# The first expert's token list in token order, two of its row tiles gathered before the last dense store, its first four slices split 256+128

## The chip, the cores and the metric

One core of a Trainium2 chip. The metric is the device time of one execution in microseconds (us). It has five engines with queues of their own, each worked off in order: PE (TensorE, matmuls), DVE (VectorE), ACT (ScalarE), POOL (GpSimd) and SP (SyncE, which here only issues transfers).

## The reference, cut to what matters

Three stages follow one another on 3072 tokens of 512 numbers:

```python
x = attention(q, k, v, mem_k, mem_v)         # windows of 32 queries, 8 heads of 64
h = x @ w_in; g = np.maximum(0.01 * h, h)    # dense: 512 -> 2048 -> 512
x = g @ w_out
logits = x @ w_gate                          # 8 experts, cap = 3072 // 8 = 384 tokens each
# (token, expert) pairs from the highest logit down: a token goes to the first expert
# of its pairs that is not full yet, until every token has one
for e in range(8):
    out[mask[e]] = np.maximum(x[mask[e]] @ w1[e], 0.0) @ w2[e]     # 512 -> 1024 -> 512
```

Every expert ends with exactly 384 tokens. Which expert fills first, and with which tokens, depends on the logits of all tokens.

## The kernel before, in words

**Order.** Nothing is written in its final order by hand. `Plan` holds every instruction (or small group) as an operation with an engine, a planned duration, a key (lower goes first) and what it depends on. A list scheduler goes through them with these durations and so sets the order of each engine's queue; the hardware then runs the queues with semaphores. A planned duration that is off costs nothing by itself, it only changes orders.

**Dense stage.** Tokens go in 8 blocks of 384 (`TB`), that is 3 row tiles of 128 (`TT`), 24 row tiles in all. The hidden 2048 are 16 slices of 128. A slice is `gemm1` (12 matmuls of 384 columns: each operand is a high and a low part, three products of four depth pieces) and `gemm2` (9 matmuls of 512 columns, three for each row tile). The plan numbers slices s = 16 * block + slice, and `gemm2` of slice s comes two slices behind `gemm1`. Attention units of 96 queries run between the slices of the block before; for the last block they are spread by `EARLY`.

**Towards the routing.** The routing needs all logits, and these can be had without the last `gemm2`s: from slice S6 = 7*16 - ND on, `gate` multiplies the hidden slice with the folded matrix w_out @ w_gate (two matmuls of 384 columns a slice, L994; the last three slices by 8-column matmuls, L1004), and what was summed up to then gives its part by dot products on DVE (`x2_part`, `x2_gate`, L1069). So the `gemm2`s from S6 on are put off (hidden slices kept in `gd`, in `spare` and in parts of `win`): those of the last ND slices of block 6, and all 16 of block 7, row tile by row tile (21, 22, 23). PE has them to do while the search runs.

**Search.** `search(p)` finds the expert that fills p-th and its tokens. It is a chain of small DVE steps and small PE steps (`count` L315, `base` L337, `sums`, `before_it`): each step waits for the one before. `fill` marks the tokens, `ranks`, `slots`, `places`, `parts`, `tokens`, `indices` turn them into a list of 384 token numbers (`tail(p)`). The slot of a token in the list is the number of list tokens in lower partitions plus those in earlier row tiles of its own partition.

**Experts.** `gather` fetches the list's rows from `x2d` (dense results in DRAM, stored by `x2_out` L1053, L1054) with three indirect transfers of 128 rows from POOL (L478), one for each row tile of the list. `transpose` (L483, 4 matmuls a row tile), `xhi` (ACT, L486) and `xlo` (DVE, L490) make the operand. An expert has 8 slices of `gemm1` (L614) and `gemm2` (L637), the same shapes as the dense ones. Its weights are loaded by SP (L587) and split in high and low by ACT (L595) and DVE (L597); those of the first expert go through the `x` buffers and into `win` (`room`), piece f once the dense slices that lie there are used up (`roomy`).

In the first expert every gather waits for every dense store (`xready`) and for `open_experts`, and every first matmul of `gemm1` waits for all three row tiles (`XT[p]`). What follows the last dense matmul is filled on PE by up to 40 matmuls of the identity (L667).

Of the kernel before, what the change touches and what calls it, by code (L numbers as in the profile page):

```python
# [67 lines left out]
class Plan:  # L68
# [37 lines left out]
    def dma(self, us, fn, deps=(), use=(), after=(), key=None, queue=0.45):  # L106
        q = self.op({"Q": queue}, fn, deps, use, after, key)
        d = self.op({"D": us}, None, (), use, (), key)
        self.dep(d, [q], lat=1.1)
        return d  # L110

    def run(self):
# [13 lines left out]
        while todo:  # L126
# [29 lines left out]
            todo -= 1  # L156
            if o.fn:
# [55 lines left out]
def phase2(tc, P, C, ident, L, x2d, we, out, ps_h, ps_o, ps_y, pools, lready, xready, open_pools, open_experts, room, roomy, before):  # L213
# [17 lines left out]
    SW = 0.12  # L231
# [171 lines left out]
    def fill(p):  # L403
# [4 lines left out]
        fx = r["fx"] = rt([128, NTILE + 1], BF, "fx", 2)  # L408
# [16 lines left out]
    def ranks(p):  # L425
        r = R[p]
        r["ps"] = pools["ps_t"].tile([128, 1], FT, name="pt")
        nc.tensor.matmul(r["ps"], C[0]["tri"], r["fx"][:, NTILE:], start=True, stop=True)

    def slots(p):  # L430

        r = R[p]
        b = rt([128, NTILE], FT, "sb")
        a = rt([128, NTILE], I16, "sl")
        V.tensor_scalar(b, r["fx"][:, :NTILE], r["ps"], 32.0, op0=OP.add, op1=OP.add)
# [45 lines left out]
    def transpose(b, x):  # L481
        for d in range(KD):
            nc.tensor.transpose(b.t[:, d * 128:(d + 1) * 128], x.t[:, d * 128:(d + 1) * 128], ident)  # L483
# [17 lines left out]
    r_xt = [ring(2, [128, KD, TB], FR, f"xt{n}") for n in "hl"]  # L501
    r_g = [ring(3, [128, TB], FR, f"eg{n}") for n in "hl"]
# [10 lines left out]
    def search(p):  # L513
# [6 lines left out]
        for n in range(NL):  # L520
# [3 lines left out]
            o = small((0.047 if n < UPPER else 0.06) * W, lambda n=n: count(p, n), [o], late=late)  # L524
# [5 lines left out]
        o = small(0.17, lambda: sums(p), [o], late=late)  # L530
        o = P.op(("V", 1.9), lambda: which(p), [o])
        t = small(0.04, lambda: before_it(p), [o], late=late)
        o = P.op(("V", 0.8), lambda: above(p), [o])
        chain[:] = [P.op(("V", 0.72), lambda: full(p), [o, t])]
        filled[p] = P.op(("V", 0.5), lambda: fill(p), chain, key=-1000 + 10 * p + (1 if p else -1))
# [3 lines left out]
    def tail(p):  # L539
        P.key = -1000 + 10 * p + (1 if p else -1)  # L540
        late = SLACK if p else 0.0
        o = small(0.04, lambda: ranks(p), [filled[p], tchain], late=late)
        o = P.op(("V", 0.67), lambda: slots(p), [o])
        ts = [P.op(("V", 0.47), lambda: places(p), [o]), P.op(("V", 0.6), lambda: parts(p), [o])]
        o = small(0.53, lambda: tokens(p), ts, late=late)
# [3 lines left out]
        for i in range(TT):  # L549
            x = r_xg[i].take()  # L550
# [724 lines left out]
```

## Time and profile before

| | |
|---|---|
| median of 3 runs | 993.36 us (993.26 to 994.73) |
| the profiled execution | 995.56 us |
| its span on the core | 993.8 us |
| PE busy | 971.8 us (98%) |
| DVE busy | 768.8 us (77%) |
| ACT busy | 444.9 us (45%) |
| POOL busy | 130.7 us (13%) |
| mean granted PE clock | 0.997 |

The profile comes from one execution, 995.56 us long, of which 993.8 us are the span from its first to its last instruction. Times of rows are us from the span's start. Matmuls overlap: a 512-column matmul is listed with 0.39 us, and the next one begins 0.23 us later, so the pace is read from starts, not from durations, and a busy PE can still run filler.

### The profile page before, as it was taken

The numbers are of one execution on the slowest core, as the hardware profiler recorded it, in microseconds if no ns is written. First come the engines' busy times: TensorE is split into PE (matmuls) and PEld (weight loads), VectorE is DVE, ScalarE is ACT, GpSimd is POOL, SyncE is SP. The second block draws the span as 40 slices with busy tenths as digits, with TensorE's granted clock in tenths as the row PEclk, the third lists the DMA queues.
The fourth block names the chain that finished last, engine by engine and source line by source line (L and its number), as shares of the span: only waits on it lengthen the run. The fifth ranks groups of instructions, "written<-read, shape, count | busy, mean of one in ns | idle before, by whom it ended". The sixth has DMA issues, their size and how long they took to land.

```text
span 993.8 us, 17323 instructions
## 1 busy us (share of the span) xinstructions
PE 971.8 (98%) x6068; PEld 844.4 (85%) x6068; DVE 768.8 (77%) x2573; ACT 444.9 (45%) x1187; POOL 130.7 (13%) x145
## 2 busy tenths in 40 slices
PE   8899999999999999999999999998999999999997
PEld 7778888888888888888888889877888888888996
DVE  7899798698698689689778685579988989885710
ACT  7777634444444544444544433214425334334521
POOL 0577521000000000000000000001121112112211
PEclk9999999999999999999999999999999999999999
DMA  8567521111011111110120000024633625526600
GB/s 262 197 213 239 191 65 30 30 62 60 30 62 39 50 63 30 56 65 31 48 72 12 1 1 1 37 75 155 201 127 129 204 94 169 172 74 209 226 32 32
DMA packets 36327, 95.50 MB, mean 96 GB/s; under 512 B 4368, under 2 KB 8464, under 8 KB 36112
## 3 DMA queue, kind: packets, MB, share of 16 engines
q1 hardware_dynamic: 32256, 81.54, 24.6%
q0 software_dynamic: 3840, 12.59, 3.8%
q8 instruction: 48, 0.79, 0.3%
q14 instruction: 39, 0.32, 0.1%
q10 hardware_dynamic: 144, 0.26, 0.1%
HBM read 81.79 MB, written 12.58 MB: 95 GB/s over the span
## 4 chain that ended last, share of the span: by engine, by line
PE 83%; DVE 8%; issue 4%; ACT 1%; DMA 1%; POOL 1%; POOLq 0%; DVEq 0%; ACTq 0%; SPq 0%
PE po L1039 24%; PE ph L946 24%; PE ph L614 13%; PE po L637 11%; PE pa L828 3%; PE pa L898 2%; PE pa L871 2%; PE po L1094 2%; DVE junk L1069 2%; DVE wp L923 1%; DVE wa L925 1%; DMA wst<-in_w_dram 1%; PE pt L483 1%; DVE wp L922 1%; PE pc L315 1%
## 5 line engine op out<-in xcount | busy, mean ns | idle before, releaser
L1069 DVE CUSTOM_DVE_ANT_0 junk<-x,wgb 128x512 bf16<-128x512 f32 x296 | 207.5, 701 | 5.6 <-ACT x L1053 0.8
L954 ACT ACTIVATE gs<-ph 128x384 f32<-128x384 f32 x128 | 62.6, 489 | 196.9 <-PE ph L946 189.9
L1039 PE MATMUL po<-wouth,gh 128*128 128x512 f32 x336 | 136.4, 406 | 0.0
L955 DVE TENSOR_TENSOR gs<-ph,gs 128x384 f32<-128x384 f32 x128 | 71.1, 555 | 84.1 <-ACT gs L954 83.8
L1039 PE MATMUL po<-woutl,gh 128*128 128x512 f32 x336 | 133.7, 398 | 1.3 <-POOL woutl L930 1.3
L1039 PE MATMUL po<-wouth,gl 128*128 128x512 f32 x336 | 132.0, 395 | 0.6 <-POOL gl L957 0.6
L837 ACT ACTIVATE X<-X,st 96x128 f32<-96x128 f32 x248 | 96.8, 391 | 47.7 <-DVE st L832 47.4
L946 PE MATMUL ph<-x1h,winh 128*128 128x384 f32 x512 | 111.5, 339 | 0.0
L946 PE MATMUL ph<-x1h,winl 128*128 128x384 f32 x512 | 110.9, 337 | 0.1
L946 PE MATMUL ph<-x1l,winh 128*128 128x384 f32 x512 | 110.3, 336 | 0.0
L946 PEld LDWEIGHTS ph<-x1h,winh 128*128 128x128 f32 x512 | 91.7, 188 | 9.5
L620 ACT ACTIVATE egh<-ph 128x384 fp32r<-128x384 f32 x64 | 31.4, 491 | 150.5 <-PE ph L614 142.2
L946 PEld LDWEIGHTS ph<-x1h,winl 128*128 128x128 f32 x512 | 92.3, 188 | 1.4 <-POOL winl L930 0.4
L946 PEld LDWEIGHTS ph<-x1l,winh 128*128 128x128 f32 x512 | 91.2, 189 | 0.2
L1039 PEld LDWEIGHTS po<-wouth,gl 128*128 128x128 f32 x336 | 63.0, 188 | 15.4 <-POOL gl L957 1.7
L1039 PEld LDWEIGHTS po<-wouth,gh 128*128 128x128 f32 x336 | 63.1, 188 | 13.7
L1039 PEld LDWEIGHTS po<-woutl,gh 128*128 128x128 f32 x336 | 63.2, 188 | 12.9 <-POOL woutl L930 2.7
L956 ACT ACTIVATE gh<-gs 128x384 fp32r<-128x384 f32 x112 | 58.7, 524 | 34.1 <-DVE gs L955 33.9
L621 DVE SCALAR_TENSOR_TENSOR egl<-ph,egh 128x384 fp32r<-128x384 f32 x64 | 35.3, 551 | 44.0 <-ACT egh L620 43.7
L832 DVE CUSTOM_DVE_ANT_0 X<-pa,masks 96x128 f32<-96x128 f32 x232 | 56.3, 281 | 4.7 <-PE pa L828 4.7
L957 DVE TENSOR_TENSOR gl<-gs,gh 128x384 fp32r<-128x384 f32 x88 | 48.5, 551 | 10.7 <-ACT gh L956 10.6
L1154 POOL IOTA ij<- 128x128 int32 x1 | 0.2, 235 | 425.7 <-DVE L L1069 425.7
(245 smaller groups left out, 1911.5 us busy)
## 6 DMA issues: line engine op xcount, KB each, us to landing
west<-in_we_dram SPq DMA_DIRECT2D x56, 512.0 KB, 4.5
wst<-in_w_dram SPq DMA_DIRECT2D x32, 512.0 KB, 4.2
vt<-in_v_dram SPq DMA_DIRECT2D x30, 256.0 KB, 2.6
kt<-in_k_dram SPq DMA_DIRECT2D x30, 256.0 KB, 3.4
qt<-in_q_dram SPq DMA_DIRECT2D x31, 192.0 KB, 3.0
x2d<-x SPq DMA_DIRECT2D x21, 256.0 KB, 2.2
x<-in_we_dram SPq DMA_DIRECT2D x16, 256.0 KB, 2.7
wgb<-in_w_gate_t_dram SPq DMA_DIRECT2D x1, 2048.0 KB
```

The costliest lines, as they stand in the source:

```text
L614: nc.tensor.matmul(ph.t[:, :TB], w[a].t[:, k * 128:(k + 1) * 128], xs[x].t[:, k, :], start=(n == 0), stop=(n == 3 * KD - 1))
L621: b = P.op(("V", 0.47), lambda: V.scalar_tensor_tensor(gl.t, ph.t[:, :TB], 0.0, gh.t.bitcast(FT), op0=OP.max, op1=OP.subtract), [a], [ph, ...
L637: nc.tensor.matmul(ACC[p][i].t, l.t[:, 128 * i:128 * i + 128], w[a].t[:, 512:1024], start=(f == 0 and n == 0), stop=(f == NF - 1 and n == 2))
L832: V.tensor_tensor_reduce(out=X.t[:, h, :], in0=ps[h % 2].t[:QB, h // 2 * 128:h // 2 * 128 + 128], in1=masks[:, var, :], scale=-scale, scal ...
L837: S.activation(X.t[:, h, :], X.t[:, h, :], AF.Exp, bias=st.t[:, 0, h:h + 1], scale=-1.0, accum_out=st.t[:, 2, h:h + 1])
L946: nc.tensor.matmul(ph.t[:, :TB], win[wt][:, f, kk * 128:(kk + 1) * 128], xt.t[:, kk, :], start=(n == 0 and kk == 0), stop=(n == 2 and kk = ...
L954: o = P.op(("S", 0.37), lambda: S.activation(t.t, ph.t[:, :TB], AF.Copy, scale=0.01), [o], [ph, t], key=k)
L955: o = P.op(("V", 0.47), lambda: V.tensor_tensor(t.t, ph.t[:, :TB], t.t, op=OP.max), [o], [ph, t], key=k)
L956: x = P.op(("S", 0.42), lambda: S.activation(gh(), t.t, AF.Copy), [o, gd], [t, *gb], key=k)
L957: y = P.op({"V": 0.47} if j > 1 else {"V": 0.47, "G": 0.96} if j else {"G": 0.96}, lambda e=V if j > 1 else G: e.tensor_tensor(gl(), t.t, ...
L1039: nc.tensor.matmul(acc.t, lt()[:, sl], wout[wt][:, f, :], start=(f == 0 and n == 0), stop=(n == 2 and (f == NF - 1 or s == S6 - 1)), skip_ ...
L1069: V.tensor_tensor_reduce(out=pools["wgb"].tile([128, DM], BF, name="junk"), in0=x, in1=WGB[0][:, e, :], scale=1.0, scalar=0.0, op0=OP.mult ...
```

## The change

1. `ranks` and `slots` number the list by token: a matmul with ones gives the count of each row tile, a scan over the row tiles and a subtraction the tokens in earlier tiles, the matmul with the triangle the rank inside the tile. This holds for all eight lists. Slot s then has a token of at most 3071 - (383 - s), so the first 128 rows of a list lie in row tiles 0 to 21 and the next 128 in 0 to 22.
2. For the first expert, gathers 0 and 1 read only `x2d` up to row tiles 21 and 22, go to a free part of the `gd` buffers (`rows`) and wait neither for later stores nor for `open_experts`. Gather 2 is as before. `open_experts` waits for the two early transposes.
3. For the first expert, slices 0 to 3 run first for the columns of row tiles 0 and 1 (256), `gemm1` and `gemm2`, then for row tile 2 (128); slices 4 to 7 follow whole. Its operands and hidden slices use the dense buffers (`mlp` stays open).
4. The identity matmuls at L667 are gone. Those of the start (`warm`) take a bank of PSUM whose users have ended in the plan, or are left out.
5. ND goes from 3 to 8 (S6 from 109 to 104): five more slices of block 6 are put off and gated, and the last block's attention units lie 2.2 instead of 3.8 slices apart. The dot products of block 6 get a later key.
6. Weight loads of the first expert no longer wait for `roomy`; the splits do, pieces 0 to 2 only for the last `gemm1`, the others for the last dense matmul as well. Some planned durations of small PE steps are lower.

```diff
 def ranks(p):
-        r["ps"] = pools["ps_t"].tile([128, 1], FT, name="pt")
-        nc.tensor.matmul(r["ps"], C[0]["tri"], r["fx"][:, NTILE:], start=True, stop=True)
+        r["ps"] = pools["ps_t"].tile([128, 2, NTILE], FT, name="pt")
+        for n, x in enumerate(("ones", "tri")):
+            nc.tensor.matmul(r["ps"][:, n], C[0][x], r["F"], start=True, stop=True)
 def slots(p):
-        V.tensor_scalar(b, r["fx"][:, :NTILE], r["ps"], 32.0, op0=OP.add, op1=OP.add)
+        V.tensor_tensor_scan(fx, r["ps"][:, 0], c["zero"], 0.0, op0=OP.add, op1=OP.add)
+        V.tensor_tensor(fx, fx, r["ps"][:, 0], op=OP.subtract)
+        V.scalar_tensor_tensor(b, r["ps"][:, 1], 32.0, fx, op0=OP.add, op1=OP.add)
 def fill(p):
-        V.memset(fx[:, 0:1], 0.0)
-        V.tensor_tensor_scan(fx[:, 1:], r["F"], c["zero"], 0.0, op0=OP.add, op1=OP.add)
 def gather(p, i, x):
-        G.indirect_dma_start(out=x.t, out_offset=None, in_=x2d,
+        G.indirect_dma_start(out=x.t if p or i == TT - 1 else x.t[:, i * DM:(i + 1) * DM], out_offset=None, in_=x2d if p else x2d[:(NTILE - TT + 1 + i) * 128],
 def tail(p):
-            g = P.op(("G", 1.25), lambda i=i, x=x: gather(p, i, x), [o, xready, open_experts], [x])
+            early = p == 0 and i < TT - 1
+            g = P.op(("G", 1.25), lambda i=i, x=x: gather(p, i, x),
+                     [o, [d for t, d in xready if p or t < NTILE - TT + 1 + i], [] if early else open_experts], [x])
...
+            if early:
+                P.dep(open_experts, [o])
 def gemm1(p, f, lo=0, hi=TB):
-            t = [P.op(("T", 0.175), lambda n=n: mm(n), [o[0], XT[p], t], [ph, *w, *xs])]
+            t = [P.op(("T", {128: 0.112, 256: 0.122, TB: 0.178}[k]), lambda n=n: mm(n),
+                      [o[0], XT[p][lo // 128:hi // 128], t], [ph, *w, *xs])]
...
-    b, o = ps_o[0].take(), before
-    for n in range(40):
-        prev, o = o, P.op(("T", 0.22), lambda: None if b.gone else nc.tensor.matmul(
-            b.t[:, :128], ident, ident, start=True, stop=True), (), [b] if n == 0 else (), key=1e6)
-        P.dep(o, [prev], lat=0.15)
...
+        if p == 0:
+            for lo, hi in ((0, TB - 128), (TB - 128, TB)):
+                tiles = range(lo // 128, hi // 128)
+                for f in range(FA + 2):
+                    if f < FA:
+                        if lo == 0:
+                            load(p, f)
+                        gemm1(p, f, lo, hi)
+                    if f >= 2:
+                        gemm2(p, f - 2, tiles)
...
-    ND = 3
+    ND = 8
...
     def warm():
-        b = next((b for b in spots[::-1] if (b.tile or b is spots[0]) and not b.gone), None)
-        if b:
-            nc.tensor.matmul(b.t[:, 384:], ident, ident, start=True, stop=True)
+        for b in spots:
+            if (b.tile or b is spots[0]) and not b.gone and all(u.end and u.end < P.now - 0.05 for u in b.users):
+                nc.tensor.matmul(b.t[:, 384:], ident, ident, start=True, stop=True)
+                break
```

## Rows read from the trace of the kernel before

**Rows 1.** The page: PE's busy time, and the chain that ended last by engine.

```profile
PE 971.8 (98%) x6068; PEld 844.4 (85%) x6068; DVE 768.8 (77%) x2573; ACT 444.9 (45%) x1187; POOL 130.7 (13%) x145
...
PE 83%; DVE 8%; issue 4%; ACT 1%; DMA 1%; POOL 1%; POOLq 0%; DVEq 0%; ACTq 0%; SPq 0%
```

**Rows 2.** Timeline of PE, 669 to 684: start, us, instruction.

```profile
669.40 0.39 PE L1039 MATMUL po<-wouth,gl 128*128 128x512 f32 x1
...
678.17 0.60 PE L483 MATMUL pt<-ident,xg 128*128 128x128 f32 x4
...
683.05 0.96 PE L614 MATMUL ph<-xth,winh 128*128 128x384 f32 x4
```

**Rows 3.** Timeline of DVE, ACT, SP and POOL, 633 to 684.

```profile
633.14 0.18 DVE L1022 TENSOR_SCALAR L<-pl 128x24 f32<-128x24 f32 x1 [0.39 <-PE pl L1004]
...
657.82 0.60 ACT L1053 ACTIVATE x1h<-po 128x512 f32<-128x512 f32 x1 [12.99 <-PE po L1039]
...
664.74 0.70 DVE L475 TENSOR_TENSOR idx<-pt,ix 32x3 int32<-32x3 f32 x4
...
669.83 0.60 ACT L1053 ACTIVATE x1h<-po 128x512 f32<-128x512 f32 x1 [3.39 <-PE po L1039]
...
670.45 0.33 SPq L1054 DMA_DIRECT2D x2d<-x1h  x1
...
673.64 1.17 POOL L478 DMA_INDIRECT xg<-x2d,idx  x1 [73.55 <-DVE d L281]
...
682.42 0.58 ACT L486 ACTIVATE xth<-ph 128x512 fp32r<-128x512 f32 x1
...
683.17 0.68 DVE L490 TENSOR_TENSOR xtl<-ph,xth 128x512 fp32r<-128x512 f32 x1
```

**Rows 4.** Groups of PE instructions by line and shape, 669.63 to 683.05: busy us, mean ns.

```profile
L483 PE MATMUL ph<-ident,xg 128*128 128x128 f32 x8 | 1.3, 280 | 0.3 <-DMA xg<-x2d,idx 0.3
L315 PE MATMUL pc<-oh,cm 128*128 128x32 bf16 x18 | 0.9, 178 | 1.4 <-DVE cm L298 0.8 <-issue 0.6
L483 PE MATMUL pt<-ident,xg 128*128 128x128 f32 x4 | 0.6, 272 | 0.0
L337 PE MATMUL pb<-fl,ones 32*128 32x1 bf16 x3 | 0.5, 158 | 1.1 <-DVE fl L333 0.7 <-issue 0.3
L315 PE MATMUL pc<-oh,cm 128*128 128x16 bf16 x12 | 0.5, 170 | 0.0
```

**Rows 5.** Timeline of PE in the first expert: the pace of 384 and 512 columns.

```profile
698.38 0.85 PE L614 MATMUL ph<-xth,winl 128*128 128x384 f32 x4
699.08 0.85 PE L614 MATMUL ph<-xtl,winh 128*128 128x384 f32 x4
699.77 0.39 PE L637 MATMUL po<-winh,egh 128*128 128x512 f32 x1
700.00 0.40 PE L637 MATMUL po<-winl,egh 128*128 128x512 f32 x1
```

**Rows 6.** Groups of PE, 575 to 635: the put-off products of block 6.

```profile
L1039 PE MATMUL po<-wouth,gd 128*128 128x512 f32 x18 | 6.1, 395 | 0.0
```

**Rows 7.** Busy time by stretch: PE, PEld, DVE, ACT, POOL, then granted clock, DMA.

```profile
520.00:540.00 20.00, 20.00 (x129) 17.87 (x128) 18.85 (x63) 8.29 (x25) 0.00 (x0) 1.00 0.05 14
540.00:560.00 20.00, 20.00 (x129) 17.86 (x128) 16.95 (x59) 8.91 (x31) 0.00 (x0) 1.00 0.00 1
...
600.00:633.00 33.00, 33.00 (x187) 30.37 (x185) 14.46 (x45) 13.73 (x28) 0.10 (x1) 0.95 0.07 24
...
721.30:918.00 196.70, 194.97 (x1189) 163.94 (x1185) 162.99 (x587) 78.40 (x150) 34.94 (x47) 1.00 0.44 148
```

**Rows 8.** The same view over single microseconds: the granted clock.

```profile
628.00:629.00 1.00, 1.00 (x6) 1.00 (x6) 0.00 (x0) 0.00 (x0) 0.00 (x0) 0.73 0.21 78
...
631.00:632.00 1.00, 1.00 (x4) 0.75 (x3) 0.56 (x1) 0.38 (x2) 0.00 (x0) 0.56 0.00 0
```

**Rows 9.** Timeline of PE: the one wait of a later expert's start.

```profile
918.14 0.97 PE L614 MATMUL ph<-xth,winh 128*128 128x384 f32 x4 [1.15 <-ACT xth L486]
```

More of the change, by code (lines that the diff above doesn't have):

```diff
@@ L109, in dma @@
         self.dep(d, [q], lat=1.1)
+        d.queue = q
         return d
@@ L156, in run @@
             todo -= 1
+            self.now = t
             if o.fn:
@@ L523, in search @@
             o = P.op(("V", 0.08 + K * T * W / 1920), lambda n=n: compare(p, n), [o])
-            o = small((0.047 if n < UPPER else 0.06) * W, lambda n=n: count(p, n), [o], late=late)
+            o = small(0.026 * W, lambda n=n: count(p, n), [o], late=late)
             for m in range(K - 1):
@@ L607, in gemm1 @@
         xs = X[p]
+        c, k = slice(lo, hi), hi - lo
         ph = ps_h.take()
-        gh, gl = (r.take() for r in r_g)
+        gh, gl = (r.take() for r in (r_gb if lo else r_g))
         def mm(n):
             a, x = ((0, 0), (1, 0), (0, 1))[n // KD]
-            k = n % KD
-            nc.tensor.matmul(ph.t[:, :TB], w[a].t[:, k * 128:(k + 1) * 128], xs[x].t[:, k, :],
+            d = n % KD
+            nc.tensor.matmul(ph.t[:, :k], w[a].t[:, d * 128:(d + 1) * 128], xs[x].t[:, d, c],
                              start=(n == 0), stop=(n == 3 * KD - 1))
@@ L630, in gemm2, with mm @@
         w, o = W[p, f]
-        gh, gl, done = GL.pop(s)
-        if f == 0:
+        if f == 0 and p not in ACC:
             ACC[p] = [r.take() for r in ps_o]
-        def mm(i, n):
+        def mm(i, n, gh, gl, at):
             l, a = ((gh, 0), (gh, 1), (gl, 0))[n]
-            nc.tensor.matmul(ACC[p][i].t, l.t[:, 128 * i:128 * i + 128], w[a].t[:, 512:1024],
+            nc.tensor.matmul(ACC[p][i].t, l.t[:, at:at + 128], w[a].t[:, 512:1024],
                              start=(f == 0 and n == 0), stop=(f == NF - 1 and n == 2))
-        for i in range(TT):
+        for i in tiles:
+            gh, gl, at, done = GL.pop((s, i))
             if p == E - 1 and f >= NF - 2:
@@ L678, in phase2 @@
         tail(p)
-        for f in range(NF + 2):
-            if f < NF:
+        first = []
+        if p == 0:
[8 more added lines that the diff above has]
+                        gemm2(p, f - 2, tiles)
+            first = range(FA)
+        for f in range(NF):
+            if f not in first:
                 load(p, f)
@@ L683, in phase2 @@
             s = NF * p + f - 2
-            if f >= 2 or p > 0:
-                if f < NF:
-                    gemm2(*divmod(s, NF))
+            if s >= 0 and s not in first:
+                gemm2(*divmod(s, NF))
         if p == E - 1:
@@ L969, in gstore @@
         if n < 0:
-            b = [r_gd.take() for _ in range(2)]
-            return (lambda: b[0].t), (lambda: b[1].t), b, [ev["gd"]]
+            if n == -ND:
+                early.extend(r.take() for r in r_gd)
+            return (lambda: early[0].t[:, n + ND, :]), (lambda: early[1].t[:, n + ND, :]), early, [ev["gd"]]
         if n < KD:
```

94 lines of the change are left out of this document (50 added, 44 removed).

## The prediction

> **What bounds the kernel now.** I read the page first: PE is busy in nearly the whole span, and the chain that ended last runs through PE for 83% of it [rows 1]. So time is won where PE waits or does filler, and lost wherever PE gets more work. A busy share doesn't show filler, so next I followed the timeline of PE through the passage from the dense stage to the experts. The last dense matmul starts at 669.40; at the pace of 0.23 us for 512 columns [rows 5] the next could start at 669.63. The first matmul of an expert starts at 683.05 [rows 2]. These 13.4 us hold no dense and no expert product.
>
> The timelines of the other engines say why [rows 3]. The search of the first expert begins when the logits are complete, at 633.14, and its list is ready after the four steps at 664.74, so at 665.4: before the dense stage ends. What ends last is the store. ACT copies the last row tile at 669.83, SP issues its store at 670.45, the first gather starts at 673.64, its rows are turned by PE at 678.17 [rows 2], and the other two row tiles follow; ACT's last copy ends at 683.00, and PE starts 0.05 us later. DVE's last low part ends at 683.85, in time for the third product.
>
> After that PE holds: from 721.3 to 918 it has gaps of 1.7 us in 196.7, DVE is busy for 163.0 of them, 83% [rows 7], and the only start of an expert that waits long is that of the seventh, 1.15 us [rows 9]. So what is won in the passage should reach the end.
>
> **What the change takes away.** Of the 13.4 us PE uses some for work that stays: transposes (1.3 + 0.6), counts (0.9 + 0.5) and bases (0.5) of the second search, 3.8 us [rows 4]. They will lie between other matmuls then. The rest, 13.4 - 3.8 = 9.6 us, is filler and waiting, and can go if three things are in time at the end of the dense stage, which I call T.
>
> The list and row tiles 0 and 1. The store of row tile 22, copied at 657.82 [rows 3], takes as long as the last one did (669.83 to 673.64, 3.8 us until a gather may start), so gather 1 could start at 661.6. The list allows 665.4 even with the old search start. And the search may start earlier: five more slices of 9 matmuls leave the time before the logits, 45 x 0.232 = 10.4 us, and 1.75 us of gating enter it (below), 8.7 us in sum, and the list would be there at 656.8. Then the row tiles are turned some 4.5 us after their gathers (673.64 to 678.17), around 661 and 666, and are operands before T. With the old search start they would be there near T + 3.
>
> The weights. Pieces 0 to 2 may be split before T, when ACT is nearly idle; piece 3 only after T, and PE wants it after three slices of 256 columns and two row tiles of one `gemm2`, about 3 x 1.44 + 1.4 = 5.7 us later. I cost that at nothing; cover gone, it is the wait for two copies on ACT (0.6 us each).
>
> Row tile 2. Its way is the old one for one tile: T + 0.2 for the copy, gather at T + 4.0, turned at T + 8.5, then transpose, copy and low part as the last tile has them now (0.6 + 0.6 + 0.7): T + 10.5. Until then PE has four slices of 256 columns and 24 products of 512, 48 x 0.12 + 24 x 0.232 = 11.3 us, and about 1 us of small steps of the second search. So it is the next to be late, with a margin of some 1.8 us. I cost it at nothing.
>
> **What the change adds on PE.**
> Splitting: 48 matmuls of 384 columns become 48 of 256 and 48 of 128. 384 columns go at 0.70 / 4 = 0.174 us, 512 at 0.232 [rows 5]: 0.058 for every 128. On this line 256 cost 0.116 and 128 cost 0.058, which would make the split free: the lower bound. But each matmul brings its own 128x128 weights, and the nearest row with 128 columns and fp32 weights, four transposes in 0.60 us with 0.27 for one [rows 2, 4], goes at 0.11. The upper bound is that a narrow matmul costs as much as one of 384: 48 x 0.174 = 8.4 us. I take 0.12 and 0.11, since the transposes are nearest: 48 x (0.23 - 0.174) = 2.7 us.
> The Trainium skill, page "TensorE: Matmul & The Clock Gate", section "Back-to-back issue gap", gives about 81 ns a matmul of 128 columns in a sustained stream of weight loads and matmuls. By it, as an estimate, the split would cost 48 x 0.029 = 1.4 us less. The same section gives 131 ns for 512 columns, which this trace contradicts with 232 ns (fp32 operands here), so I stay with the transposes.
> Gates: five slices more, two matmuls of 384 columns each: 10 x 0.174 = 1.75 us. Ranks: one more matmul of 24 columns for each of eight lists, at most the 0.05 us of a count's matmul (0.9 / 18) [rows 4]: 0.4 us.
> On DVE the lists need one more small step each, and the first four slices two evictions instead of one; DVE has 17% to spare [rows 7], so I cost that at nothing on the path.
> Orders: in the 256-column stretch `gemm1` goes through two banks of PSUM, each freed by ACT and then DVE, and DVE's queue has steps of the second search in it. A slice now takes 1.4 us on PE instead of 2.1, so a late eviction shows. Nothing in the trace prices it; from 0 to 3 us, I take 0.8, less than one step of 0.68 on DVE [rows 3] for each second slice.
> Other edits: the later experts' start can only lose its wait of 1.15 us; search and experts both move earlier, so I take half, 0.6. `warm` acts in the first 30 us, before the weights' splitting sets the pace: nothing, and 1 us either way if not.
>
> **Sum.** 9.6 - 2.7 - 1.75 - 0.4 - 0.8 + 0.6 = 4.55 us less. The profiled execution was 995.56 us with a span of 993.8, which is 2.2 above the median of the runs; the difference is taken off the median: 993.36 - 4.55 = 988.8 us.
>
> **The rivals.**
> A better one: narrow matmuls on the line (2.7 less), no order loss (0.8 less) and the whole 1.15: 993.36 - (9.6 - 1.75 - 0.4 + 1.15) = 984.8. For it: the planner's order hid nearly all else. Against it: the 0.11 of the transposes.
> A late start: the logits don't come earlier, because PE does the put-off products first. All 27 of them ran between 575 and 635 (shown are the 18 of two of the three products, [rows 6]), before the logits were complete, presumably because PE had nothing else ready. If the 72 go the same way, row tiles 0 and 1 are operands near T + 3: 988.8 + 3 = 991.8. Against it: DVE has 18 us to spare from 600 to 633 [rows 7], and the dot products that held the slices up get a later key.
> The clock: just before the search, after 8-column matmuls, the granted clock was 0.73 in the first of four microseconds, 0.50 in two and 0.56 in the last [rows 8]: a fall from 2.4 to 1.2 GHz that cost 0.27 + 0.5 + 0.5 + 0.44 = 1.7 us. The filler at L667 went through the present gap at full clock. If row tile 0 or 2 leaves PE waiting 2 us without filler, the same drop adds 1.7: 988.8 + 3.7 = 992.5.
> The Trainium skill, the same page, section "Why this matters for your kernels", warns against idle stretches between bursts of matmuls for this reason; it speaks against taking the filler out, and the trace bears out the drop, not yet its place.
> The other side: the last block's attention. Its four units go from 3.8 to 2.2 slices apart while blocks' dot products run on DVE, which is busy for 35.8 of 40 us from 520 to 560 already [rows 7]. If DVE can't be packed closer, the logits of block 7 and all that follows don't come earlier while the products are moved out from between: PE then idles for up to the 10.4 us moved, 993.36 - 4.55 + 10.4 = 999.2. It makes the kernel slower from 6.6 us of such idling on. Against it: gates and folds can slip past 600, and put-off products fill PE.
>
> **How the numbers follow.** Chances: the forecast with its bounds (986.4 to 990.9) 0.58; the better one 0.15; the late start 0.10; the clock 0.07; the attention 0.10. About 2 us, 0.2%, is what a measurement of this kernel can tell from no change: faster is below 991.4, slower above 995.3. Faster: 0.58 + 0.15 + half the late start = 0.78. Slower: 0.09 of the attention's 0.10. The rest, 0.13, is within. The range goes from the better case, 984.5, to the clock's, 992.8, and leaves out the attention and a little below.
>
> **What would show it.** Right: no L667, `gemm1` at L614 within 1 us of the last L1039; two gathers before that and one some 4 us after; in the first 20 us of the expert pairs of starts 0.12 and 0.11 us apart; the first step of the search near 624; PE granted 1.00 throughout. Wrong: PE waiting for `xth` between the 256- and the 128-column stretch, 128 columns at over 0.15 us, gaps on PE between 480 and 560, or an expert past the second starting after a wait longer than 1.15 us.

## The result, and the profile after

The changed kernel takes 1000.61 us (median of 10 runs, 997.19 to 1004.14) where the kernel before takes 993.89 us (10 runs): a ratio of 1.0066, interval 1.005 to 1.0083. The forecast was 988.8 us, and even its range ended at 992.8. The profiled execution of the change has a span of 999.0 us. The page looks as before [rows 1]: PE is 5.3 us busier, and its share of the chain is the same.

```profile
PE 977.1 (98%) x6070; PEld 846.1 (85%) x6070; DVE 771.6 (77%) x2577; ACT 443.3 (44%) x1191; POOL 130.0 (13%) x145
...
PE 83%; DVE 8%; issue 4%; DMA 2%; ACT 1%; POOL 1%; POOLq 0%; SPq 0%; DVEq 0%; ACTq 0%
```

The first expert now starts as predicted. The timeline of PE around it, to be held against [rows 2] (the dense products are L1058 now, the experts' first products L624):

```profile
671.05 0.40 PE L1058 MATMUL po<-wouth,gl 128*128 128x512 f32 x1
671.28 0.63 PE L624 MATMUL ph<-x1h,winh 128*128 128x256 f32 x4
671.75 0.64 PE L624 MATMUL ph<-x1h,winl 128*128 128x256 f32 x4
...
683.81 0.60 PE L487 MATMUL pt<-ident,xg 128*128 128x128 f32 x4
685.10 0.66 PE L624 MATMUL ph<-x1h,winh 128*128 128x128 f32 x4 [0.69 <-ACT x1h L490]
...
686.25 0.61 PE L624 MATMUL ph<-x1l,winh 128*128 128x128 f32 x4
686.69 0.61 PE L624 MATMUL ph<-x1h,winh 128*128 128x128 f32 x4
...
690.41 0.33 PE L624 MATMUL ph<-x1h,winh 128*128 128x128 f32 x1 [1.69 <-DVE egbl L633]
```

The first expert follows the last dense product with no gap, 11.8 us earlier than in [rows 2]. Four products of 256 columns take 0.47 us, four of 128 take 0.44. But behind the third tile's transposes PE waits 0.69 us for their copy, and at 690.41 it waits 1.69 us for DVE's eviction of a narrow slice. That eviction starts at 690.07, behind steps of the second list's end in DVE's queue (688.89 to 690.03); DVE is busy for 4.71 of the 5 us from 685 to 690. No filler stands in PE's waits any more. The view over stretches of 5 us (PE, PEld, DVE, ACT, POOL, then granted clock, DMA) shows what came of it, and the same twice again later:

```profile
690.00:695.00 5.00, 4.59 (x35) 4.50 (x35) 4.67 (x22) 1.31 (x3) 2.21 (x2) 0.68 0.64 239
695.00:700.00 5.00, 5.00 (x19) 3.95 (x19) 2.02 (x6) 1.83 (x4) 1.09 (x2) 0.64 0.65 238
840.00:845.00 5.00, 5.00 (x16) 4.55 (x17) 2.90 (x11) 1.53 (x3) 0.00 (x0) 0.50 0.02 5
885.00:890.00 5.00, 5.00 (x16) 4.55 (x17) 4.81 (x12) 2.36 (x5) 0.00 (x0) 0.52 0.00 0
```

From 690 to 700 the granted clock is at 0.68 and 0.64 of its 2.4 GHz level, which costs by estimate 5 x 0.32 + 5 x 0.36 = 3.4 us. From 840 to 845 and from 885 to 890 it is at its 1.2 GHz level, 2.5 and 2.4 us; with the slices of 5 us beside them (0.86 and 0.96; 0.79) these two falls come to 3.4 us each as well, at most: PE is idle for 2.4 and 2.8 us of the slices ahead, and what the clock was then counts for nothing. The timeline of PE at the fifth and sixth expert's starts shows what stands ahead of them; before, only the seventh expert had such a wait [rows 9]:

```profile
836.31 0.63 PE L487 MATMUL pt<-ident,xg 128*128 128x128 f32 x4 [1.19 <-issue]
...
837.78 1.01 PE L624 MATMUL ph<-x1h,winh 128*128 128x384 f32 x4 [0.59 <-ACT x1h L490]
...
839.64 0.34 PE L318 MATMUL pc<-oh,cm 128*128 128x32 bf16 x6 [0.53 <-DVE cm L301]
...
880.38 0.66 PE L487 MATMUL pt<-ident,xg 128*128 128x128 f32 x4 [0.47 <-DVE lc L325]
881.80 0.16 PE L340 MATMUL pb<-fl,ones 32*128 32x1 bf16 x1 [0.77 <-DVE am L333]
883.19 1.09 PE L487 MATMUL pt<-ident,xg 128*128 128x128 f32 x4 [1.23 <-issue]
...
884.97 1.65 PE L624 MATMUL ph<-x1h,wh 128*128 128x384 f32 x4 [0.38 <-ACT x1h L490]
```

These are the transposes of the next expert's rows, done so late that PE has nothing else left while it waits from one tile to the next: in each of the three waits of 0.47, 1.19 and 1.23 us the transposes start 0.1 us after DVE's low part of the tile before ends (880.32, 836.21, 883.09). The rows are late for PE because the list is. In the timeline of POOL, the first gather of some lists, first before, then in the change:

```profile
703.01 0.94 POOL L478 DMA_INDIRECT xg<-x2d,idx  x1 [25.67 <-DVE egl L621]
...
742.69 0.99 POOL L478 DMA_INDIRECT xg<-x2d,idx  x1 [11.83 <-issue]
...
860.67 0.99 POOL L478 DMA_INDIRECT xg<-x2d,idx  x1 [12.36 <-issue]
```

```profile
652.65 1.51 POOL L482 DMA_INDIRECT gdl<-x2d,idx  x1 [69.65 <-DVE cm L301]
660.35 1.02 POOL L482 DMA_INDIRECT gdl<-x2d,idx  x1 [6.19 <-DMA x2d<-gdh]
676.29 1.14 POOL L482 DMA_INDIRECT xg<-x2d,idx  x1 [14.92 <-ACT winh L604]
692.49 1.34 POOL L482 DMA_INDIRECT xg<-x2d,idx  x1 [15.06 <-DVE lc L325]
...
738.90 0.99 POOL L482 DMA_INDIRECT xg<-x2d,idx  x1 [11.71 <-issue]
...
867.93 0.99 POOL L482 DMA_INDIRECT xg<-x2d,idx  x1 [29.47 <-PE ph L624]
```

(The first three lines of the change are the first expert's three tiles; the others are the second, third and sixth list, in both.) The first gather comes 21 us earlier than in [rows 3]; there it waited for the last store, its list was ready at 665.4, so the list itself is some 13 us earlier. The second is 10.5 us ahead, the third 3.8, the fifth is level (821.99 for 822.00, with PE 2.6 us ahead), and the sixth is 7.3 us behind. The experts' starts tell the same: the first is 11.8 us earlier than before, the second 6.8, the fifth 2.6, and the sixth 7.6 us later. The second expert's first products, before and in the change:

```profile
721.34 0.95 PE L614 MATMUL ph<-xth,wh 128*128 128x384 f32 x4
```

```profile
714.52 0.87 PE L624 MATMUL ph<-x1h,wh 128*128 128x384 f32 x4
```

The first loss is in the narrow stretch. In the timeline of DVE a step of the third list's search has its flags at 694.56, and their product comes 4 us later, since PE's queue has the slow products of the third row tile ahead of it:

```profile
694.56 0.14 DVE L336 TENSOR_SCALAR fl<-am 32x1 bf16<-32x1 f32 x1
698.57 0.27 DVE L284 SCALAR_TENSOR_TENSOR d<-km,pb,zero 128x48 bf16<-128x48 int32 x1 [2.18 <-PE pb L340]
```

After 714.5 the kernel loses 12.0 us to the one before (6.8 ahead at the second start, 5.2 behind at the last scatter, 993.26 for 988.02). PE idles 121.5 - 120.6 + 45.0 - 43.0 + 41.0 - 38.6 = 5.2 us between 714.5 and 922, against 1.7 in [rows 7]: 3.5 us more. The two falls of the clock are up to 6.9 us. The remaining 1.6 us or more I can't place.

```profile
714.50:836.00 121.50, 120.63 (x740) 100.81 (x738) 100.68 (x366) 45.25 (x88) 21.12 (x30) 1.00 0.43 145
836.00:881.00 45.00, 43.01 (x251) 35.10 (x252) 35.99 (x134) 14.99 (x30) 6.95 (x10) 0.92 0.37 126
881.00:922.00 41.00, 38.62 (x216) 33.84 (x215) 28.76 (x92) 14.52 (x28) 4.89 (x7) 0.92 0.42 141
```

### The profile page after: what moved, and what is told of

The parts are those of the page before. It is cut to its first block, busy times and chain, and to the rows that moved or that the text cites. A ratio compares the mean times of both kernels' runs of the same rounds, so it can differ in the third digit from the quotient of the medians.

```text
span 999.0 us, 17323 instructions
## 1 busy us (share of the span) xinstructions
PE 977.1 (98%) x6070; PEld 846.1 (85%) x6070; DVE 771.6 (77%) x2577; ACT 443.3 (44%) x1191; POOL 130.0 (13%) x145
## 4 chain that ended last, share of the span: by engine, by line
PE 83%; DVE 8%; issue 4%; DMA 2%; ACT 1%; POOL 1%; POOLq 0%; SPq 0%; DVEq 0%; ACTq 0%
PE po L1058 24%; PE ph L964 23%; PE ph L624 13%; PE po L649 11%; PE pa L846 3%; PE pa L916 2%; PE pa L889 2%; DVE junk L1088 2%; DMA wst<-in_w_dram 1%; DVE wp L941 1%; DVE wa L943 1%; PE po L1113 1%; DVE wp L940 1%; PE pt L487 1%; PE pc L318 1%
## 5 line engine op out<-in xcount | busy, mean ns | idle before, releaser
L1058 PE MATMUL po<-wouth,gh 128*128 128x512 f32 x321 | 130.7, 407 | 0.6 <-ACT wouth L947 0.5
L1058 PE MATMUL po<-woutl,gh 128*128 128x512 f32 x321 | 127.8, 398 | 1.6 <-POOL woutl L948 1.6
L1058 PE MATMUL po<-wouth,gl 128*128 128x512 f32 x321 | 126.3, 395 | 0.9 <-POOL gl L975 0.8
L631 ACT ACTIVATE gh<-ph 128x384 fp32r<-128x384 f32 (+1 forms) x64 | 31.0, 485 | 157.7 <-PE ph L624 139.0
L1058 PEld LDWEIGHTS po<-wouth,gl 128*128 128x128 f32 x321 | 60.3, 188 | 15.1 <-POOL gl L975 2.2
L1058 PEld LDWEIGHTS po<-wouth,gh 128*128 128x128 f32 x321 | 60.3, 188 | 14.5 <-ACT wouth L947 0.8
L1058 PEld LDWEIGHTS po<-woutl,gh 128*128 128x128 f32 x321 | 60.4, 188 | 12.8 <-POOL woutl L948 3.0
L974 ACT ACTIVATE gh<-gs 128x384 fp32r<-128x384 f32 x107 | 56.1, 524 | 32.1 <-DVE gs L973 32.0
L633 DVE SCALAR_TENSOR_TENSOR gl<-ph,gh 128x384 fp32r<-128x384 f32 (+1 forms) x64 | 34.9, 546 | 39.7 <-ACT gh L631 39.2
L975 DVE TENSOR_TENSOR gl<-gs,gh 128x384 fp32r<-128x384 f32 x83 | 45.8, 552 | 9.4 <-ACT gh L974 9.3
```

The source lines that it names most:

```text
L633: b = P.op(("V", 0.47), lambda: V.scalar_tensor_tensor(gl.t[:, :k], ph.t[:, :k], 0.0, gh.t[:, :k].bitcast(FT), op0=OP.max, op1=OP.subtract ...
L974: x = P.op(("S", 0.42), lambda: S.activation(gh(), t.t, AF.Copy), [o, gd], [t, *gb], key=k)
L975: y = P.op({"V": 0.47} if j > 1 else {"V": 0.47, "G": 0.96} if j else {"G": 0.96}, lambda e=V if j > 1 else G: e.tensor_tensor(gl(), t.t, ...
L1058: nc.tensor.matmul(acc.t, lt()[:, sl], wout[wt][:, f, :], start=(f == 0 and n == 0), stop=(n == 2 and (f == NF - 1 or s == S6 - 1)), skip_ ...
```

## The experiments

Three things could have cost the time: the waits of the 128-column part, with the clock that falls there and holds up a search (theory A); the planner's new durations, a dozen of them in the diff, most for steps of a search or a list's end, some lower and some higher than before, of which the prediction priced none (theory B); or the experts' own work (theory D). All kernels are the changed one with one edit, unless said otherwise. The kernel before took 993.9 us beside the change and 994.8 to 995.3 beside the experiments, so differences in us to the change are uncertain by about 1 us and mostly too small; the ratios are all to the kernel before, measured beside each.

**Matmuls of the identity in the narrow stretch (`fill_narrow`).** All queues keep their order; the fillers write columns of a bank that nothing else uses.

```
+    def keep_warm(count):
+        for _ in range(count):
+            nc.tensor.matmul(DONE[-1].t[:, 384:], ident, ident, start=True, stop=True)
...
+            if p == 0 and f == 0 and i == TT - 1 and n == 1:   # in gemm2's mm
+                keep_warm(8)
...
+        if x is xg0[0]:                                        # in transpose, third tile
+            keep_warm(4)
```

> The changed kernel with every queue in the same order, and 12 matmuls of the identity added on PE where the 128-column part of the first expert waits: 4 behind the transposes of the third tile (its wait was 0.69 us), 8 behind the first slice's second product with 128 columns (its wait was 1.69 us); at 0.23 us each they fill those waits and cost at most 0.4 us more. Theory A (the waits of the 128-column part let the granted clock fall to 0.68 and 0.64 in 690 to 700; that costs 3.4 us, holds up the step of the second search that stands in PE's queue there, and makes the later lists late): the clock stays at 1.00 there, the second expert starts near 711 instead of 714.5, the lists of the fifth and sixth expert are in time, their two falls of the clock are gone too, 987 to 991 us. Theory B (the lists are late because a search takes longer than an expert in this order, wherever it starts): only the first fall goes, the later waits grow by what was gained, 997 to 1000 us. Theory C (the clock falls for something other than these waits): the fall stays, 1000 to 1002 us.

Measured: 995.48 us, ratio to before 1.001 (1.0 to 1.0021), between the ranges of theories A and B. The fillers take the place of the waits, and the clock holds, first in this kernel's timeline of PE, then in its stretches:

```profile
683.33 1.06 PE L619 MATMUL ph<-ident 128*128 128x128 f32 x8
...
687.63 2.05 PE L619 MATMUL ph<-ident 128*128 128x128 f32 x16
689.47 0.33 PE L633 MATMUL ph<-x1h,winh 128*128 128x128 f32 x1
```

```profile
690.00:695.00 5.00, 5.00 (x40) 4.40 (x40) 4.63 (x21) 3.15 (x7) 2.84 (x3) 1.00 0.52 177
695.00:700.00 5.00, 5.00 (x34) 4.60 (x32) 4.84 (x14) 2.15 (x5) 0.45 (x1) 1.00 0.83 308
```

Theory C is out: the same products, in the same order, with the waits filled, run at full clock. The second expert starts at 710.45, as theory A said. (The step held up in the narrow stretch is of the third list's search, not the second's as the expectation has it.) But the later lists still come late (the sixth at 861.4), the waits at the fifth and sixth start are there again, and so is a fall at the sixth. So A accounts for some 5 us, and something else, perhaps B, for the rest.

**Fillers at the fifth and sixth start (`fill_late`).**

```
...
+                if p in (4, 5) and i:
+                    keep_warm(5)
                 transpose(b, xg[i], i * DM if early else 0)
+                if p in (4, 5) and i == TT - 1:
+                    keep_warm(3)
```

> The changed kernel with every queue in the same order, and 13 matmuls of the identity added on PE in each of the fifth and sixth expert's starts: 5 ahead of the second and 5 ahead of the third tile's transposes, 3 behind them. At 0.23 us each they are 3.0 us for waits of 2.3 and 2.9 us. Theory A and B (the waits let the clock fall, and each fall costs 3.4 us): no fall at 840 to 845 and 885 to 890, the narrow stretch as before, 1000.6 - 6.8 + about 1 = 994 to 996 us. Theory C (the falls have another cause): they stay, 1001 to 1003 us.

Measured: 997.48 us, ratio 1.0025 (1.0014 to 1.0037): 3.1 us less than the change (4.1 by the ratios), where theories A and B said 4.6 to 6.6. The clock is at 1.00 in both places:

```profile
840.00:845.00 5.00, 4.11 (x29) 3.53 (x27) 4.49 (x14) 2.42 (x6) 1.09 (x1) 1.00 0.30 110
885.00:890.00 5.00, 4.30 (x35) 3.76 (x34) 4.87 (x12) 2.30 (x5) 0.00 (x0) 1.00 0.00 0
```

So these falls come from the waits too. Their worth I had too high: with the clock up, PE reaches its next search product earlier and waits there (0.74 us for DVE at 842.41), and 13 fillers are 3.0 us for waits of 2.3 and 2.9. The profiled execution, the slowest of eight, also has a larger fall in the narrow stretch (the second expert starts at 716.3 for 714.5).

**The planner's numbers as before (`plan_numbers`).**

```
-    SW = 0.08
+    SW = 0.12
-            o = small(0.026 * W, lambda n=n: count(p, n), [o], late=late)
+            o = small((0.047 if n < UPPER else 0.06) * W, lambda n=n: count(p, n), [o], late=late)
...
```

> The changed kernel with the planned durations of the search, of the transposes and of the experts' products as they were before (0.12 us a semaphore wait, 0.047 and 0.06 us a count, 0.53 us for the tokens and so on), so that the planner orders the later searches as if they took longer; the early tiles, the token order and the split stay. Theory B (the new planned durations put the search's steps where they come late): the lists keep their lead, no late waits at the fifth and sixth expert, 988 to 992 us. Theory A (the narrow stretch makes them late): the narrow stretch stays and so do late waits, 997 to 1003 us.

Measured: 989.54 us, ratio 0.9939 (0.9915 to 0.9963): faster than both kernels. No fall of the clock between 640 and 960, neither in the narrow stretch nor later. Theory B holds: with the old numbers the passage's gain reaches the end, and the narrow stretch keeps its full clock too.

**Rows gathered with a list that is there (`rows_one_list_early`).**

```
-                             in_offset=bass.IndirectOffsetOnAxis(ap=R[p]["idx"][:, i:i + 1], axis=0))
+                             in_offset=bass.IndirectOffsetOnAxis(ap=R[max(p - 1, 0)]["idx"][:, i:i + 1], axis=0))
...
-        o = small(0.06, lambda: ranks(p), [filled[p], tchain], late=late)
+        if p == 0:
+            listed()          # ranks, slots, tokens, indices; for p > 0 after the transposes
```

> The changed kernel, but from the second expert on an expert's rows are gathered with the list of the expert before it (the searches and lists are all computed and the results scattered with the right list; what is left out is that the rows are the expert's own), so that no expert has to wait for its own list. Theories A and B (late lists make the experts' starts wait and the clock fall, 2 x 6.4 us): the waits at the fifth and sixth start and their falls of the clock are gone, the narrow stretch keeps its own, 987 to 991 us. Theory D (the experts' products take longer in this order, and the late lists only follow PE): 997 to 1001 us.

Measured: 986.06 us, ratio 0.9916 (0.9899 to 0.9933). PE's longest wait after 660 is 0.7 us, the clock is at 1.00 from 600 to 960, and the numbers of the planner are still the new ones. So theory D is out: with rows on time the experts lose nothing, which fits late lists as the way in which the numbers cost time. By itself it doesn't part them from the narrow stretch, though: the edit also moves the end of a list behind the transposes, and against the expectation the narrow stretch has no fall here either (its second wait is 0.54 us). The rows are not the expert's own, so this is only a mark of what is to be had: some 9 us against the kernel before.

**The numbers in groups.** Each group of planned durations alone went back to its old values.

```
-    SW = 0.08                                          # sw_back
+    SW = 0.12
-            o = small(0.026 * W, ...                   # counts_back, with sums and before_it
+            o = small((0.047 if n < UPPER else 0.06) * W, ...
-        o = small(0.17, lambda: tokens(p), ...         # tail_back, with fill, ranks, slots
+        o = small(0.53, lambda: tokens(p), ...
-        ... TB: 0.178}[k] ... ("T", 0.235) ...         # pace_back, with the transposes
+        ... TB: 0.175}[k] ... ("T", 0.231) ...
```

> The changed kernel with one planned duration as it was before: 0.12 us instead of 0.08 for the wait around every small product of a search. Theory B1 (planned too short, each small product comes into PE's queue late for the search, so the lists of the fourth to sixth expert come 43 us apart instead of 39): this number stands in every step, so it gives most of the 11 us of all numbers together, 989 to 993 us. Theory B2 (no one number does it: the changed kernel's order is one unlucky order among many, and any other number gives another): 989 to 995 us here, and about the same from the other three groups.

> The changed kernel with the planned durations of the counts (0.047 and 0.06 us a product instead of 0.026), the sums (0.17 for 0.10) and the ties (0.04 for 0.02) as before. Theory B1: these make a step 0.13 to 0.4 us longer in the plan, six steps a list: half or more of the 11 us, 990 to 995 us. Theory B2: 989 to 995 us, as any other group.

> The changed kernel with the planned durations of a list's end as before (fill 0.5, ranks 0.04, slots 0.67, tokens 0.53 us). Theory B1 (the steps of the search matter): these stand once a list and not in its steps, so the late lists stay, 997 to 1001 us. Theory B2: 989 to 995 us, as any other group.

> The changed kernel with the planned durations of the experts' own work as before (transposes 0.44, products 0.175 and 0.231 us). They differ by 2% and touch no step of a search. Theory B1: late lists stay, 997 to 1001 us. Theory B2: 989 to 995 us, as any other group.

Measured: 987.72, 991.06, 997.98 and 1000.67 us; ratios 0.9924 (0.9901 to 0.9946), 0.9957 (0.9946 to 0.9969), 1.0029 (1.0017 to 1.0041) and 1.005 (1.0031 to 1.0068). That is theory B1 in its order: the one number that stands in every step of a search is worth 12.9 us, the counts 9.5, a list's end 2.6, the experts' pace nothing that can be told from no change. It stands in 19 products a list: 14 of the search, two of the list's end and three tiles' transposes. The shares don't add up: all numbers together give 11.1 us, less than the one alone. Theory B2, by which any group would do, falls with the last two.

**The same number, other values.** 0.16 us, 0.10 and 0.04; and 0.08 in the kernel before.

> The changed kernel with 0.16 us planned for the wait around every small product of a search (the change has 0.08; with 0.12 it took 987.7 us). In the trace of the change a threshold product on PE costs 0.20 us of the other products' pace (676.26 to 676.94, of which four products of 256 columns are 0.475), where the plan has 0.03 + 0.08. Theory B1 (planned too short is what hurts): 0.16 does as well as 0.12, 986 to 990 us. Theory B3 (the value 0.12 only happens to give a good order): any value as likely as another, 994 to 1000 us here.

> The changed kernel with 0.10 us planned for that wait. Theory B1: between, 989 to 998 us. Theory B3: anything, so 1000 us or more is as likely as 988 us.

> The changed kernel with 0.04 us planned for the wait around a small product (0.08 took 1000.6, 0.12 took 987.7, 0.16 took 988.6 us). Theory B1 (too short is what hurts): as slow or slower, 1000 to 1006 us. Theory B3 (0.08 is only an unlucky order): 988 to 998 us.

> The kernel before with that one number changed, 0.12 to 0.08, and nothing else. Theory B1: its lists, 39.4 us apart as the experts are, come later by a like amount as in the change (up to 4 us each), and once the lead is gone its experts wait too: 997 to 1002 us. Theory B4 (the number hurts only together with the early start, which leaves the lists less lead): 993 to 996 us, no difference to the kernel before.

Measured: 988.63 us for 0.16 (0.9935, 0.9919 to 0.9952), 990.81 for 0.10 (0.995, 0.9934 to 0.9967), 999.04 for 0.04 (1.0038, 1.0025 to 1.0051). So 0.10 and above is good, 0.08 and below is bad: not one unlucky order (B3 falls). But 0.04 is no worse than 0.08, and 1 us under theory B1's range. In the kernel before, 0.08 did no harm, 993.59 us (0.9985, 0.9974 to 0.9995), and its lists are not slower. That is the time of theory B4, but not its reason, since there was no slowness for a longer lead to hide. That kernel still has the old durations of the counts, which alone mend most of the change too (`counts_back`).

**Where the missing time is planned.**

```
-            t = [P.op(("T", {128: 0.112, 256: 0.122, TB: 0.178}[k]), ...    # pace_longer
+            t = [P.op(("T", {128: 0.112, 256: 0.122, TB: 0.182}[k]), ...    # and 0.240 for 0.235
-    LATE, SLACK = 0.3, 0.7                                                  # late_034
+    LATE, SLACK = 0.34, 0.74
```

> The changed kernel with its 0.08 us, but the experts' own products planned 2% longer (0.182 and 0.240 us instead of 0.178 and 0.235): that adds some 0.8 us to an expert in the plan, as much as 0.04 us on about 19 small products. Theory B1a (the plan's PE is ahead of the chip's, on whichever product): 988 to 993 us. Theory B1b (the small products' own place is what matters): 997 to 1003 us.

> The changed kernel with its 0.08 us, but every small product of the later searches planned 0.04 us later after what it needs (0.34 and 0.74 us instead of 0.3 and 0.7), which takes no time of PE in the plan. Theory B1b (the arrival matters): 988 to 994 us. Theory B1a (PE's time in the plan matters): 997 to 1003 us.

Measured: 992.36 us (0.9969, 0.9956 to 0.9981) and 997.74 us (1.0027, 1.0014 to 1.0041). Time on PE's products mends 8.3 of the 12.9 us, a later arrival mends 2.9. B1a is nearer: it is PE's time in the plan that is too short, on whichever product. The kernel's text agrees: the number makes a small product longer on PE in the plan, and the step that needs its result is planned that much before its end (`early=SW`), so it is not put off. In the changed kernel's timeline of PE a threshold's product has this price:

```profile
676.26 0.64 PE L624 MATMUL ph<-x1l,winh 128*128 128x256 f32 x4
676.83 0.17 PE L340 MATMUL pb<-fl,ones 64*128 64x1 bf16 x1
676.94 0.50 PE L649 MATMUL po<-winh,gl 128*128 128x512 f32 x1
677.27 0.40 PE L649 MATMUL po<-winh,gh 128*128 128x512 f32 x1
```

From 676.26 to 676.94 are 0.68 us; the four wide products alone go in 0.47. So it takes 0.2 us ahead of the next product, and that one's successor starts 0.33 us after it instead of 0.23: 0.3 us of PE in all, where the change plans 0.03 + 0.08 and the kernel before 0.03 + 0.12. There are six of these in a list, so the change's plan is short by some 6 x 0.19 = 1.1 us a list, an estimate. Yet the old numbers are no truer: a count of six products takes 0.25 us (it starts at 700.74, the next products at 700.90 and 701.22), the change plans 0.24, the kernel before 0.40. What they gave the plan is more time of PE.

**Two other parts, with 0.12 us (`sw_back_no_split`, `sw_back_nd3`).** `FA = 0` leaves the first expert whole; `ND = 3` holds back three dense slices as before, with the old key of the dot products.

> With 0.12 us again, and the first expert's first four slices whole (384 columns), so that it starts when its third tile is there. The third tile's transposes end near 684 and the dense products near 672.5, which leaves PE about 11 us where the split kernel waits 2.9 us once; the split itself cost 2.7 us by the prediction. Theory P (the prediction's passage holds): 987.7 + 8 - 2.7 = 993 us, and 996 to 997 us if the granted clock falls after that gap as well. Theory Q (the split buys nothing, since the lists set the later starts): 987 to 989 us.

> With 0.12 us again, and the last 3 dense slices held back as before instead of 8 (the gates of the earlier tokens come ahead of the held products again, the two early tiles and the split stay). By the prediction the 8 gave 1.75 us and let the first list be done early enough; the plan has the first gather 13 us later. Theory P: 989.5 to 992 us. Theory Q (the lists' lead over the later experts matters more than the start): with the lists later by 10 us late waits come back, 995 to 1000 us.

Measured: 999.41 us (1.0036, 1.0022 to 1.005) and 993.49 us (0.9981, 0.997 to 0.9993). Without the split PE waits 9.9 us from 665 to 700, and the clock is at its lower level from 675 to 690 (0.52, 0.50 and 0.50 in three stretches, of which this is the middle one):

```profile
680.00:685.00 5.00, 2.17 (x7) 1.41 (x7) 4.87 (x21) 1.81 (x4) 0.00 (x0) 0.50 0.61 170
```

So the split, with the early start that it allows, is worth 11.7 us, more than theory P's 5 to 9. With three slices the first gather comes at 661.65, some 10 us later than with eight, and the kernel loses 5.8 us, a little beyond theory P; but it keeps its later lists in time, so theory Q falls for both.

**All in one table.** "Lists" is the time from the second list's first gather to the sixth's; at the experts' pace of before, 196.8 / 5 = 39.4 us from the second start to the seventh, four take 157.4. "DVE on PE" is the time that DVE waited for a product of PE from 690 to 900 in the view of waits. The clock is the lowest granted in stretches of 20 us, up to 960.

| kernel | us | lists | DVE on PE | clock 680 to 700 | clock after 700 |
|---|---|---|---|---|---|
| before | 993.9 | 157.7 | 12.0 | 1.00 | 1.00 |
| change | 1000.6 | 175.4 | 20.7 | 0.83 | 0.83 |
| pace_back | 1000.7 | 172.4 | 23.4 | 0.68 | 0.84 |
| sw_004 | 999.0 | 169.6 | 23.3 | 0.83 | 0.87 |
| tail_back | 998.0 | 172.1 | 22.8 | 0.74 | 0.84 |
| late_034 | 997.7 | 170.6 | 22.6 | 0.67 | 0.91 |
| fill_late | 997.5 | 175.5 | 20.0 | 0.69 | 0.97 |
| fill_narrow | 995.5 | 169.8 | 20.1 | 1.00 | 0.90 |
| pace_longer | 992.4 | 166.6 | 18.7 | 0.74 | 1.00 |
| counts_back | 991.1 | 164.5 | 17.1 | 0.84 | 0.99 |
| sw_010 | 990.8 | 164.1 | 15.9 | 0.70 | 0.95 |
| sw_back_nd3 | 993.5 | 158.7 | 15.8 | 1.00 | 1.00 |
| sw_back_no_split | 999.4 | 160.0 | 18.8 | 0.69 | 1.00 |
| before_sw_008 | 993.6 | 156.5 | 11.7 | 0.91 | 1.00 |
| plan_numbers | 989.5 | 161.0 | 13.6 | 1.00 | 1.00 |
| sw_016 | 988.6 | 157.5 | 13.7 | 0.91 | 1.00 |
| sw_back | 987.7 | 159.4 | 12.8 | 1.00 | 1.00 |

The last six have lists near the experts' pace; of them the three above 990 have lost their time before 700, by a late first expert or, in `sw_back_nd3`, by waits ahead of it and a clock of 0.74 from 660 to 680. In the rest, what mends the time mostly mends the lists too (`fill_late` mends only the clock), and the time that DVE waits for PE roughly goes with both. In the view of DVE's waits from 690 to 900, the change first, then `sw_back`:

```profile
DVE lc L325 <- PE pc L318: 7.6, 10, 1.3
DVE v L347 <- PE pb L340: 4.3, 5, 0.9
DVE d L284 <- PE pb L340: 3.8, 4, 2.2
DVE gl L633 <- ACT gh L631: 2.9, 5, 1.3
```

```profile
DVE gl L633 <- ACT gh L631: 8.0, 8, 2.6
...
DVE lc L325 <- PE pc L318: 2.4, 4, 1.0
```

In the change a search's steps wait most for their counts (7.6 us), which stand in PE's queue behind experts' products; in `sw_back` they wait 2.4 us for these, and DVE waits most for ACT ahead of evictions, which no step of a list waits for.

## Why the prediction was wrong

**What held.** The first product of an expert directly behind the last dense one (671.05 to 671.28). The gates' price: the dense end moved from 669.63 to 671.28, 1.65 us for the forecast 1.75. The paces: 0.47 / 4 = 0.118 us and 0.44 / 4 = 0.11 us for the 0.12 and 0.11 taken, so the split costs 48 x (0.228 - 0.174) = 2.6 us of PE, and no run gave the narrow products the price of either bound. The early logits (617.8 for some 624) and the two early tiles (gathers at 652.65 and 660.35). With one planned number back, the change takes 7.6 us off the kernel before (995.28 to 987.72 on one chip), 3 us more than the sum of 4.55. There the second expert starts at 713.26, 8.1 us earlier than before, and the last scatter is 7.9 us earlier (980.12): the passage was under-, not overrated, and its gain can reach the end.

The Trainium skill, page "TensorE: Matmul & The Clock Gate", section "Back-to-back issue gap", gives about 81 ns for a matmul of 128 columns; here it took 110 ns, so the trace was the better guide.

**The step that failed: "So what is won in the passage should reach the end", with "the later experts' start can only lose its wait of 1.15 us; search and experts both move earlier".** Before, four lists took 157.7 us and four experts 157.4, because, as I read it, the steps of a search stand between the experts' products in PE's queue: a list is as late as that order makes it. I took the order for given, as if everything behind the passage would only move forward, and did not price the planned durations in the diff, which write it anew. With them four lists take 175.4 us. With one of these durations back, they take 159.4 us and the kernel 987.7. Two of the signs that I wrote would show me wrong came: the wait between the wide and the narrow stretch, and a wait over 1.15 us at an expert past the second, 1.19 us at the fifth and 1.23 at the sixth (2.3 and 2.9 us with the small waits beside them).

**The clock was a rival with the right mechanism, a wrong size and too small a chance.** "If row tile 0 or 2 leaves PE waiting 2 us without filler": row tile 2 left 0.69 us, and the eviction of its first slice 1.69 behind that. The price was 3.4 us, not 1.7, and a fall came three times, up to 10.2 us; I gave it 0.07. The Trainium skill, the same page, section "Why this matters for your kernels", warns of idle stretches between bursts; here `fill_narrow` bears it out, with the same work at 1.00 once the waits were filled.

**Row tile 2.** I had it ready at T + 10.5, against 12.3 us of other work. Its gather came at 676.29, T + 5.0 for the forecast T + 4.0. PE turned it without a wait, but only at T + 12.5, behind all the products of the wide part; so nothing was left to cover its copy: 0.69 us for what I costed at nothing. The term "orders" had the right mechanism, an eviction late behind steps of a list in DVE's queue, but for the wrong stretch and too small: 1.69 us in the narrow part, where I took 0.8 for the wide one. The 17% that DVE has to spare is an average; from 685 to 690 it was 4.71 us of 5 busy. Filling the two waits, which keeps their length and saves the clock, gave 5.1 us (`fill_narrow`).

**What is shown and what isn't.** Shown: the narrow stretch's waits lower the clock (`fill_narrow`, 5.1 us); the wait planned around a small product makes the later lists late (0.04 to 0.16, and `sw_back`), and planned time on other products of PE mends most of that (`pace_longer`); the experts' own work isn't slower (`rows_one_list_early`). Shown too: that late lists cost the rest. In `pace_longer`, `counts_back` and `sw_010` the narrow stretch keeps its 1.1 to 1.8 us wait and its fall of the clock (0.74, 0.84 and 0.70 from 680 to 700), yet with lists of 164 to 167 us and no fall after 720 they are 8.3 to 9.8 us faster than the change. Only argued: that a plan with too little time on PE puts the experts' products ahead of counts which are ready sooner than PE gets there. The waits of DVE on PE fit it (20.7 against 12.8 us), but no run changed one product's place alone.

## What to carry to other kernels

When a change moves one chain forward, look at the other chains that feed what follows: one that keeps up in the profile may do so by the order of a queue, with nothing to spare. A hand-written planner's durations are part of a kernel: if they are touched, price them, and try them alone. A busy share over a long stretch, like DVE's 83%, says nothing of the few us where a new order puts everything at once. And where a filler is taken out, look for the waits that are left without one: here the clock took back 3.4 us behind two short ones.

## What the runs showed of the hardware

A wait's length alone does not tell whether the clock falls. In the change 0.69 and 1.69 us within 6 us were enough for 3.4 us of loss. In `counts_back` a single wait of 1.78 us at the same eviction was enough: the clock is at 0.87 from 690 to 695 and 0.50 from 695 to 700. But in `sw_back` PE waits 2.94 us in one piece, 7 us earlier and behind wide products, and the clock stays at 1.00. Nor did the seventh expert's 1.15 us [rows 9] lower it, nor 1.61 and 1.96 us at later experts in `sw_back_no_split`. Nor is such a wait always harmless: in `sw_016` the same eviction holds up PE for 2.95 us, behind the same kind of products, and the clock falls to 0.68. The timeline of PE and the stretches, first in `sw_back`, then in `sw_016`:

```profile
683.20 0.50 PE L624 MATMUL ph<-x1h,winh 128*128 128x256 f32 x2 [2.94 <-DVE gl L633]
```

```profile
680.00:685.00 5.00, 2.06 (x17) 1.80 (x16) 4.86 (x23) 1.50 (x4) 0.00 (x0) 1.00 0.73 191
685.00:690.00 5.00, 5.00 (x43) 4.58 (x43) 4.75 (x19) 1.54 (x5) 0.00 (x0) 1.00 0.96 360
```

```profile
681.15 0.74 PE L624 MATMUL ph<-x1h,winh 128*128 128x256 f32 x4 [2.95 <-DVE gl L633]
```

```profile
680.00:685.00 5.00, 3.85 (x18) 3.63 (x19) 4.02 (x17) 1.29 (x4) 0.00 (x0) 0.68 0.86 284
```

What makes the difference no run settles.
